# S4D convolution and gated GLU on one core: input spectrum moved once, exchanged copy on ScalarE, six more weight blocks on split parts

## The chip, the core and the metric

The kernel runs on one core of a Trainium2 chip. Its engines work side by side, each through its own list of instructions in a fixed order: TensorE (PE) multiplies, VectorE (DVE), ScalarE (ACT) and GpSimd (POOL) do elementwise work, SyncE (SP) issues the transfers between DRAM and the on-chip memory (SBUF; the products of PE land in PSUM). An instruction waits on semaphores for what it reads, and what stands behind it in its engine's list waits with it.

The metric is the time of one execution in device microseconds. A profiled execution gives the start and the duration of every instruction; the lines L1423 and so on are lines of the kernel's source.

## What is computed

A sequence of 2048 rows of 448 channels goes through a long convolution (a diagonal state space model, S4D) and through a gated linear unit; a sigmoid gate mixes the two.

```python
def _A_ref(u, log_A_real, A_imag, C_real, C_imag, log_dt, D_skip):
    ...
    P = jnp.exp((A * dt[:, None])[:, :, None] * pos[None, None, :])
    K = 2.0 * jnp.einsum("dn,dnl->dl", C, P).real
    ...
    Kf = jnp.fft.rfft(K, L2)
    Uf = jnp.fft.rfft(u_t, L2)
    y = jnp.fft.irfft(Uf * Kf[None, :, :], L2)[:, :, :L]
    ...
def _B_ref(x, w_gate, w_up, w_down):
    g = jnp.einsum("bsd,df->bsf", x, w_gate)
    u = jnp.einsum("bsd,df->bsf", x, w_up)
    h = _sigmoid(g) * u
    return jnp.einsum("bsf,fd->bsd", h, w_down)
...
g = _sigmoid((x * gate_w).sum(-1, keepdims=True))
return g * a + (1 - g) * b
```

Here D = 448, N = 256 states, L = 2048, and the hidden width of the unit is 1792 = 14 blocks of 128.

## The kernel before

**The convolution kernel K** is made in 28 chunks of 16 channels (`kgen`), each in two halves of 128 states (`half_chunk`). PE writes the angles to PSUM (L1232) and takes the whole turns off (L1241); ACT rounds and takes sines (L1236, L1238, L1243, L1244, L1254) into a tile `cs`; POOL raises powers in `tb`; DVE forms outer products of these (L1261, twice a half) and multiplies them into `cs` (L1275 and L1278). When both halves are done, PE sums over the states (L1290, 64 instructions), and ACT copies the sum out (L1311). There are three `cs` buffers. Below, "the first contraction" is L1290 of the first chunk, and the stages of the program are cut at the ends of the 1st, 9th, 20th and 28th contraction.

**The transforms** treat the 2048 rows as a matrix of 64 by 32. `Chain` holds one half of the channels: `stage1` (L812, L815), an exchange of axes (through DRAM, or on DVE, L826), `spectrum_four` (L845). For the input the spectrum is evacuated by ACT (L762) and stored in DRAM as `us` by `spectrum_u`. For the kernel there is one chain per half, tiles `fx_fu` and `fx_fk`; after the last chunk `product` goes through 8 blocks in each chain: it loads a block of `us` into a tile `ua` (`uax_fk` in the first chain, `ua_fk` in the second; two buffers each), DVE multiplies it by the kernel's spectrum straight from PSUM (L879), PE transforms back with 16 small matmuls (L889), and ACT evacuates (L762). `back` (L924, L928) makes the rows of the output.

A complex product needs real and imaginary parts against both parts of the other factor. In `us` the real parts lie in partitions 0 to 31 and 64 to 95 and the imaginary parts in the others. The kernel before writes two planes to DRAM: one with the real parts in the places of both, one with the imaginary parts in both (each transfer reads its source twice over), and `product` loads both planes of a block, in two transfers of 448 KB.

**The gated unit (GLU)** goes over 2 halves of the rows (H), 14 weight blocks (f) and 2 pieces of 512 rows (B). All operands are split in a rounded part and the rest, so that fast matmuls keep the precision. `glu_up` runs three matmuls for each of three pieces of the contraction and two for the fourth (L1423 to L1428), for gate and up; ACT takes the tanh (L1407), DVE forms the product with the up part. `glu_down` multiplies by the rows of `w_down`. Here stand two forms. For a block f that `WHOLE[H]` lists, DVE writes the product once as float32 (L1409), the weights are loaded as they are, and one float32 matmul of 448 columns is used (L1443; the profile has two records for each). For any other block DVE writes to `sg` (L1412), ACT makes the rounded part `hh` (L1414), DVE the rest `hl` (L1415), the weights are split too (L1388 on ACT, L1390 on DVE), and three fast matmuls are used (L1445, L1446, L1447). Results are scaled and added to `ob` by ACT (first group, L1455) or DVE (L1462).

**The order** is written out: the table `PLACE` gives, for each engine and each kind of tile, the places of its instructions in the engine's list. `Plan.order` merges these lists into one program; it can neither change the order on an engine nor skip a wait. So where a place in the table says that an instruction of ACT comes before another, it does, whether its input is there or not.

Of the kernel before, what the change touches and what calls it, by code (L numbers as in the profile page):

```python
# [13 lines left out]
AF = mybir.ActivationFunctionType  # L14
# [6 lines left out]
HD = 224  # L21
# [8 lines left out]
    ('Act', 'aci', 19): (65, 94,),  # L30
    ('Act', 'acr', 10): (15, 39, 49,),
    ('Act', 'acr', 19): (63, 91, 101,),
# [26 lines left out]
    ('Act', 'dots', 1): (28,),  # L59
    ('Act', 'dots', 2): (45,),  # L60
    ('Act', 'dots', 16): (67, 83,),
# [18 lines left out]
    ('Act', 'idn', 10): (12,),  # L80
    ('Act', 'junk', 10): (29, 60,),
    ('Act', 'junk', 19): (77, 81, 132,),
# [620 lines left out]
def gated_mix(ctx: ExitStack, tc, u, ut, aim, cre, cim, ldt, dskip, gw,  # L703
# [13 lines left out]
    def dt_(shape, name):  # L717
        return Res(name=name, real=dram.tile(list(shape), F32, name=name))
# [870 lines left out]
```

## Time and profile before

| what | value |
| --- | --- |
| three timed runs | 689.95, 688.12, 686.70 us; median 688.12 us |
| the profiled execution | 684.96 us |
| its span, first to last instruction | 683.0 us |
| mean granted TensorE clock | 0.999 |
| moved by DMA | 122.79 MB |

The profile's page lists the busy time of each engine, a chain of the work that ended last, and groups of instructions with their count, busy time and mean duration. A busy time is the union of the instructions' spans, and neighbours on DVE and ACT overlap a little, so that two of them in a row take less than the sum of their durations. For PE the ends are modelled, and the distance from one start to the next is the better measure. The windows give busy times of a stretch, with the number of records in brackets.

### The profile page before, as it was taken

The numbers are of one execution on the slowest core, as the hardware profiler recorded it, in microseconds if no ns is written. First come the engines' busy times: TensorE is split into PE (matmuls) and PEld (weight loads), VectorE is DVE, ScalarE is ACT, GpSimd is POOL, SyncE is SP. The second block draws the span as 40 slices with busy tenths as digits, with TensorE's granted clock in tenths as the row PEclk, the third lists the DMA queues.
The fourth block names the chain that finished last, engine by engine and source line by source line (L and its number), as shares of the span: only waits on it lengthen the run. The fifth ranks groups of instructions, "written<-read, shape, count | busy, mean of one in ns | idle before, by whom it ended". The sixth has DMA issues, their size and how long they took to land.

```text
span 683.0 us, 16235 instructions
## 1 busy us (share of the span) xinstructions
PE 669.7 (98%) x6568; PEld 480.6 (70%) x6568; DVE 603.7 (88%) x699; ACT 509.7 (75%) x928; POOL 269.2 (39%) x280
## 2 busy tenths in 40 slices
PE   8899999999999999999989999999999999999997
PEld 7677667877886687776646666778878766546864
DVE  7998999999899999999998999999974379667976
ACT  6588799898999999999999999999842442333110
POOL 0506486555466656675856567643000000000000
PEclk9999999999999999999999999999999999999999
DMA  8869432683793999737977884343968981888855
GB/s 265 222 146 245 111 101 57 174 217 139 208 173 85 204 203 225 237 111 178 176 211 179 200 212 113 124 155 111 204 133 217 280 292 66 300 276 217 153 141 129
DMA packets 96898, 122.79 MB, mean 180 GB/s; under 512 B 31032, under 2 KB 80504, under 8 KB 95800
## 3 DMA queue, kind: packets, MB, share of 16 engines
q1 hardware_dynamic: 96824, 121.76, 69.7%
q8 instruction: 52, 0.85, 0.5%
q14 instruction: 22, 0.18, 0.1%
HBM read 78.16 MB, written 43.58 MB: 178 GB/s over the span
## 4 chain that ended last, share of the span: by engine, by line
PE 82%; DVE 10%; ACT 3%; DMA 2%; issue 2%; SPq 1%; DVEq 0%
PE gu_gps L1423 10%; PE gu_gps L1424 9%; PE gu_gps L1425 9%; PE kp_egp L1290 7%; PE dn_gps L1443 6%; PE dn_gps L1445 5%; PE tp_egp L1232 4%; PE tp_egp L1241 4%; PE dn_gps L1446 4%; PE dn_gps L1447 4%; PE fps_fups L812 3%; PE gu_gps L1427 3%; PE fps_fups L845 3%; PE gu_gps L1428 3%; PE fps_fups L889 2%; PE fps_fkps L889 2%
## 5 line engine op out<-in xcount | busy, mean ns | idle before, releaser
L1423 PE MATMUL gu_gps<-xs_glu,wh_glu 128*128 128x512 f32 x336 | 144.6, 430 | 1.6 <-DVE hl_glu L1409 0.8
L1278 DVE TENSOR_TENSOR cs_eg<-cs_eg,es_eg 128x2048 f32<-128x2048 f32 x56 | 131.5, 2349 | 1.4
L1424 PE MATMUL gu_gps<-xs_glu,wh_glu 128*128 128x512 f32 x336 | 132.0, 393 | 0.1
L1425 PE MATMUL gu_gps<-xs_glu,wl_glu 128*128 128x512 f32 x336 | 131.7, 392 | 0.0
L1222 POOL TENSOR_TENSOR tb_eg<-tb_eg 128x96 f32<-128x96 f32 (+2 forms) x84 | 118.8, 1416 | 6.1
L1261 DVE TENSOR_TENSOR es_eg<-tb_eg 128x1024 f32<-128x1024 f32 x112 | 110.4, 1013 | 2.1 <-POOL tb_eg L1222 0.5
L1423 PEld LDWEIGHTS gu_gps<-xs_glu,wh_glu 128*128 128x128 f32 x336 | 63.2, 188 | 30.8 <-issue 15.8
L1275 DVE TENSOR_TENSOR cs_eg<-cs_eg,es_eg 128x1024 f32<-128x1024 f32 x56 | 70.8, 1264 | 8.2 <-ACT cs_eg L1254 5.8
L1238 ACT ACTIVATE nn_eg<-cs_eg 128x512 fp32r<-128x512 f32 x112 | 74.9, 669 | 3.8 <-PE tp_egp L1241 2.6
L1407 ACT ACTIVATE sg_glu<-gu_gps 128x512 f32<-128x512 f32 x56 | 34.5, 615 | 55.2 <-PE gu_gps L1428 54.9
L1424 PEld LDWEIGHTS gu_gps<-xs_glu,wh_glu 128*128 128x128 f32 x336 | 63.3, 188 | 16.0 <-issue 5.0
L1425 PEld LDWEIGHTS gu_gps<-xs_glu,wl_glu 128*128 128x128 f32 x336 | 63.1, 188 | 14.4
L1243 ACT ACTIVATE cs_eg<-tp_egp 128x512 f32<-128x512 f32 x112 | 70.0, 636 | 3.1 <-PE tp_egp L1241 2.7
L1236 ACT ACTIVATE cs_eg<-tp_egp 128x512 f32<-128x512 f32 x112 | 69.9, 633 | 2.7 <-PE tp_egp L1232 1.0
L1244 ACT ACTIVATE cs_eg<-tp_egp 128x512 f32<-128x512 f32 x112 | 69.0, 627 | 1.1 <-PE tp_egp L1241 1.1
L1254 ACT ACTIVATE cs_eg<-cs_eg,half_pi 128x1024 f32<-128x1024 f32 x56 | 66.7, 1191 | 0.2
L1225 POOL TENSOR_TENSOR tb_eg<-tb_eg,bs_eg 128x32 f32<-128x32 f32 x84 | 62.6, 745 | 6.4
L1462 DVE SCALAR_TENSOR_TENSOR ob_glu<-dn_gps,og,ob_glu 128x448 f32<-128x448 f32 x70 | 47.4, 677 | 16.0 <-PE dn_gps L1447 15.1
L1290 PEld LDWEIGHTS kp_egp<-cs_eg 128*32 128x32 f32 x3584 | 51.3, 110 | 10.7 <-issue 7.6
L1212 POOL MEMSET tb_eg<- 128x96 f32 x28 | 8.0, 287 | 127.9 <-DVE es_eg L1261 124.8
L1290 PE MATMUL kp_egp<-cs_eg 128*32 128x64 f32 x3584 | 55.8, 220 | 0.0
L1241 PE MATMUL tp_egp<-nn_eg,idn 128*128 128x512 f32 x112 | 51.4, 459 | 1.2 <-ACT nn_eg L1238 1.2
(168 smaller groups left out, 1326.0 us busy)
## 6 DMA issues: line engine op xcount, KB each, us to landing
shf<-fx_fu SPq DMA_DIRECT2D x16, 896.0 KB, 5.4
fx_fu<-shf SPq DMA_DIRECT2D x16, 896.0 KB, 10.4
us<-fx_fu SPq DMA_DIRECT2D x16, 896.0 KB, 9.7
xr_glu<-in_w_dram SPq DMA_DIRECT2D x46, 256.0 KB, 6.1
uax_fk<-us SPq DMA_DIRECT2D x16, 448.0 KB, 4.3
ua_fk<-us SPq DMA_DIRECT2D x16, 448.0 KB, 6.0
xr_glu<-in_w_dram SPq DMA_DIRECT2D x17, 224.0 KB, 4.1
gt_pre<-in_u_dram SPq DMA_DIRECT2D x8, 448.0 KB, 6.9
```

The costliest lines, as they stand in the source:

```text
L1222: pool(96 * m, lambda n=n, m=m: G.tensor_mul(g3(n + 1, m), g3(1, m), g3(n, 1).to_broadcast([128, 32, 3, m])))
L1236: op("Act", c_act(512, True), lambda: S.activation(cs[:, 1, ds, 32:96], block(tp), AF.Copy, bias=MAGIC), [tp], [(cs, ("s", i))], prio)
L1238: op("Act", c_act(512), lambda: S.activation(block(nn), cs[:, 1, ds, 32:96], AF.Copy, scale=-1.0, bias=MAGIC), [(cs, ("s", i))], [nn], prio)
L1241: op("PE", c_mm(532), lambda: T.matmul(tp.real, idn.real, nn.real, start=False, stop=True, skip_group_check=True), [nn, idn], [tp], prio)
L1243: op("Act", c_act(512, True), lambda: S.activation(cs[:, 0, ds, 32:96], block(tp), AF.Abs), [tp], [(cs, ("c", i))], prio)
L1261: V.tensor_mul(o.rearrange("p d (i k) -> p d i k", k=ny), x.unsqueeze(3).to_broadcast([128, 16, nx, ny]), y.unsqueeze(2).to_broadcast([128 ...
L1275: op("DVE", c_dve(1024), lambda: V.tensor_mul(cs[:, :, :, 0:32], cs[:, ::-1, :, 63:31:-1], es[:, :, 0:32].unsqueeze(1).to_broadcast([128, ...
L1278: op("DVE", c_dve(2048), lambda: V.tensor_mul(cs[:, :, :, 32:96], cs[:, :, :, 32:96], es[:, :, 32:96].unsqueeze(1).to_broadcast([128, 2, 1 ...
L1290: T.matmul(kp[32 * j:32 * j + 32, q], cs[:, z, 4 * j + q, 64:96], cs[:, z, 4 * j + q, 0:64], start=cs is parts[0] and z == 0 and q == 0, s ...
L1423: T.matmul(p.real, wh[:, k, cs], x[:, k], start=(k == 0), stop=False)
L1424: T.matmul(p.real, wh[:, k, cs], x[:, 4 + k], start=False, stop=False)
L1425: T.matmul(p.real, wl[:, k, cs], x[:, k], start=False, stop=False)
```

## The change

1. `spectrum_u` stores the spectrum once, as it lies in SBUF: 4 transfers a chain in place of 8, all of about 900 KB. `product` loads one plane of a block (one transfer of 448 KB in place of two). A new function `turn_parts` makes the second plane: for each of the two column groups z of a block, four ACTIVATE copies of 32 partitions by 448, each from one group of 32 partitions to its neighbour. That is 8 copies for a block and 128 in all. The matrices of the inverse transform change their signs to suit; sizes and numbers of the matmuls stay.
2. `WHOLE` loses blocks 11, 12 and 13 in both halves. Their 48 down products go from one float32 matmul to three of the split form. Each of the 12 pairs of block and piece gets an `hh` copy on ACT and an `hl` subtraction on DVE; the three weight blocks, shared by both halves, get a split on both engines.
3. All of `PLACE` is new.

```diff
 PLACE = {
...
-    ('Act', 'hh', 21): (237, 256, 268, 316, 333, 341,),
+    ('Act', 'hh', 21): (248, 265, 270, 318, 320, 344, 383, 401, 408, 483, 486, 494, 543, 551, 576, 647, 658, 663,),
...
-WHOLE = ((0, 1, 2, 3, 4, 11, 12, 13), (11, 12, 13))
+WHOLE = ((0, 1, 2, 3, 4), ())
...
-    turned[re], turned[im] = inv[im], -inv[re]
+    turned[re], turned[im] = inv[im], inv[im]
+    inv[im] = -inv[re]
...
-    us = [dt_([128, 2, 8, 2 * D], f"us{h}") for h in halves]
+    us = [dt_([128, 8, 2 * D], f"us{h}") for h in halves]
...
-            for q in range(2):
-                for g in range(2):
-                    for c in range(2):
-                        dma(lambda q=q, g=g, c=c: us[64 * g:64 * g + 64, c, 4 * q:4 * q + 4].rearrange(
-                                "(z k) b f -> k z (b f)", z=2),
-                            lambda q=q, g=g, c=c: x[64 * g + 32 * c:64 * g + 32 * c + 32, 16 * q:16 * q + 16].rearrange(
-                                "k l d -> k (l d)").unsqueeze(1).to_broadcast([32, 2, 8 * D]),
-                            64 * 16 * HD * 4, self.keys(8 * q, 8 * q + 8), [(us, (q, g, c))], prio, 215.0, 1400.0)
+            for q in range(4):
+                dma(lambda q=q: us[:, 2 * q:2 * q + 2].rearrange("p b f -> p (b f)"),
+                    lambda q=q: x[:, 8 * q:8 * q + 8].rearrange("p l d -> p (l d)"), 128 * 8 * HD * 4,
+                    self.keys(4 * q, 4 * q + 4), [(us, q)], prio)
...
                 ua = self.tile("ua", (128, 2, 2, D))
+                dma(lambda ua=ua: ua[:, 0].rearrange("p z f -> p (z f)"), lambda b=b: us[:, b], 128 * 2 * D * 4,
+                    [(us, b // 2)], [(ua, (0, 0)), (ua, (0, 1))], self.prio)
                 for c in range(2):
-                    dma(lambda ua=ua, c=c: ua[:, c].rearrange("p z f -> p (z f)"), lambda b=b, c=c: us[:, c, b],
-                        128 * 2 * D * 4, [(us, (b // 4, g, c)) for g in range(2)], [(ua, (c, 0)), (ua, (c, 1))], self.prio)
+                    self.turn_parts(ua, c)
                 self.product_four(ua, b)
 
+        def turn_parts(self, ua, z):
+
+            def f():
+                for a in range(0, 128, 32):
+                    to = a ^ 32
+                    S.activation(ua[to:to + 32, 1, z], ua[a:a + 32, 0, z], AF.Copy)
+            op("Act", 4 * c_act(D), f, [(ua, (0, z))], [(ua, (1, z))], self.prio)
```

In the changed kernel a line above the new function has a number lower by one than before, and a line below it a number higher by four: L1443 became L1447, L1415 became L1419.

The first place is DVE's list at the 19th chunk, both halves of it: `es` and `cs` belong to the kernel's generation, L1409 is the product of a whole block. Before:

```order
L1261 TENSOR_TENSOR es_eg_4445<-tb_eg_4240 128x16x64
L1261 TENSOR_TENSOR es_eg_4445<-tb_eg_4240 128x16x32
L1275 TENSOR_TENSOR cs_eg_4409<-cs_eg_4409,es_eg_4445 128x32x32
L1278 TENSOR_TENSOR cs_eg_4409<-cs_eg_4409,es_eg_4445 128x32x64
L1409 SCALAR_TENSOR_TENSOR hh_glu_4571<-sg_glu_4560,gu_gps_4422 128x512
L1261 TENSOR_TENSOR es_eg_4578<-tb_eg_4240 128x16x64
L1261 TENSOR_TENSOR es_eg_4578<-tb_eg_4240 128x16x32
L1275 TENSOR_TENSOR cs_eg_4528<-cs_eg_4528,es_eg_4578 128x32x32
L1278 TENSOR_TENSOR cs_eg_4528<-cs_eg_4528,es_eg_4578 128x32x64
```

In the changed kernel the list at the same chunk reads as follows; L1419 makes `hl`, and L1360 and L1361 split a piece of the input.

```order
L1419 TENSOR_TENSOR hl_glu_4548<-sg_glu_4085,hh_glu_4435 128x512
L1360 TENSOR_TENSOR xs_glu_3990<-xr_glu_3378,xs_glu_3990 128x256
L1361 TENSOR_TENSOR xs_glu_3990<-xr_glu_3378,xs_glu_3990 64x256
L1265 TENSOR_TENSOR es_eg_4624<-tb_eg_4343 128x16x64
L1419 TENSOR_TENSOR hl_glu_4642<-sg_glu_4439,hh_glu_4546 128x512
L1265 TENSOR_TENSOR es_eg_4624<-tb_eg_4343 128x16x32
L1279 TENSOR_TENSOR cs_eg_4479<-cs_eg_4479,es_eg_4624 128x32x32
L1282 TENSOR_TENSOR cs_eg_4479<-cs_eg_4479,es_eg_4624 128x32x64
L1265 TENSOR_TENSOR es_eg_4686<-tb_eg_4343 128x16x64
L1265 TENSOR_TENSOR es_eg_4686<-tb_eg_4343 128x16x32
L1279 TENSOR_TENSOR cs_eg_4633<-cs_eg_4633,es_eg_4686 128x32x32
L1282 TENSOR_TENSOR cs_eg_4633<-cs_eg_4633,es_eg_4686 128x32x64
```

Two subtractions, which the kernel before has nowhere between the 9th and the 20th contraction, stand in the first half of the chunk.

The second place is PE's list shortly ahead of the 19th contraction: `tp` and `nn` belong to the generation, `gu` to the up products, `dn` to the down products. Before:

```order
L1443 MATMUL dn_gps_4373<-vh_glu_3307,hh_glu_4571 128x448
L1241 MATMUL tp_egp_4585<-nn_eg_4605,idn 128x512
L1423 MATMUL gu_gps_4589<-xs_glu_3835,wh_glu_2408 128x512
L1424 MATMUL gu_gps_4589<-xs_glu_3835,wh_glu_2408 128x512
L1425 MATMUL gu_gps_4589<-xs_glu_3835,wl_glu_2424 128x512
```

And in the changed kernel:

```order
L1449 MATMUL dn_gps_4510<-vh_glu_3204,hh_glu_4546 128x448
L1450 MATMUL dn_gps_4510<-vh_glu_3204,hl_glu_4642 128x448
L1451 MATMUL dn_gps_4510<-vl_glu_3394,hh_glu_4546 128x448
L1236 MATMUL tp_egp_4709<-pos_sb,phs 128x512
L1245 MATMUL tp_egp_4683<-nn_eg_4704,idn 128x512
L1427 MATMUL gu_gps_4678<-xs_glu_3990,wh_glu_2793 128x512
```

The one float32 product is now three matmuls of the split form, and it reads `hl`, which the second subtraction above has made.

The third place is ACT's list in the middle of the products of the two chains. Before, evacuations follow one another, with a piece of the gated unit in between:

```order
L762 ACTIVATE fx_fk_6562<-fps_fkps_7023 128x448
L762 ACTIVATE fx_fk_6562<-fps_fkps_7022 128x448
L762 ACTIVATE fx_fu_5091<-fps_fups_7057 128x448
L762 ACTIVATE fx_fu_5091<-fps_fups_7056 128x448
L762 ACTIVATE fx_fk_6562<-fps_fkps_7070 128x448
L762 ACTIVATE fx_fk_6562<-fps_fkps_7069 128x448
L1407 ACTIVATE sg_glu_7132<-gu_gps_7005 128x512
```

In the changed kernel (evacuations are L761, the new copies L877):

```order
L877 ACTIVATE uax_fk_7173<-uax_fk_7173 32x448 x4
L761 ACTIVATE fx_fk_6687<-fps_fkps_7198 128x448
L877 ACTIVATE uax_fk_7173<-uax_fk_7173 32x448 x4
L1411 ACTIVATE sg_glu_7240<-gu_gps_7185 128x512
L761 ACTIVATE fx_fk_6687<-fps_fkps_7197 128x448
L877 ACTIVATE ua_fk_7216<-ua_fk_7216 32x448 x4
L761 ACTIVATE fx_fu_4915<-fps_fups_7244 128x448
L761 ACTIVATE fx_fu_4915<-fps_fups_7245 128x448
L877 ACTIVATE ua_fk_7216<-ua_fk_7216 32x448 x4
```

Eight copies for each block stand between the evacuations. The first of them wait for the block's transfer, and the evacuations behind them wait too.

How many instructions stand between the ends of the contractions 1, 9, 20 and 28, before and after, is this for the kinds that change on PE and DVE (instructions, not records). On PE the stages are cut behind the contraction, on DVE behind the last L1278 of the chunk.

| engine, kind | 1 to 9 | 9 to 20 | 20 to 28 | behind 28 |
| --- | --- | --- | --- | --- |
| PE whole down products (L1443) | 0, 0 | 31, 0 | 17, 0 | 0, 0 |
| PE split down products, three matmuls each | same | 9, 42 | 24, 39 | same |
| PE up products of 512 columns | -2 | +11 | -7 | -2 |
| PE angles of 512 columns (L1232) | same | +1 | -1 | same |
| PE spectrum matmuls (L845) | -4 | +4 | -4 | +4 |
| DVE `hl` subtractions (L1415) | 11, 10 | 0, 10 | 6, 9 | same |
| DVE splits of weights (L1390) | -1 | +4 (three of 448, one of 512) | same | same |
| DVE products L1409 and L1412 | same | 10, 11 | 9, 8 | same |

Ahead of the first contraction nothing changes in these numbers. Behind the 28th, DVE's list has the same kinds and numbers before and after, and ACT's has the 128 copies more. Behind the 9th contraction and up to the 28th, ACT gets the 12 `hh` copies and the three splits of weights.

More of the change, by code (lines that the diff above doesn't have):

```diff
@@ L29 @@
     ('Act', 'aci', 10): (14, 40,),
-    ('Act', 'aci', 19): (65, 94,),
-    ('Act', 'acr', 10): (15, 39, 49,),
-    ('Act', 'acr', 19): (63, 91, 101,),
[26 rows of a table removed]
-    ('Act', 'dots', 1): (28,),
+    ('Act', 'aci', 19): (61, 96,),
+    ('Act', 'acr', 10): (13, 39, 48,),
+    ('Act', 'acr', 19): (68, 91, 107,),
[26 rows of a table added]
+    ('Act', 'dots', 1): (29,),
     ('Act', 'dots', 2): (45,),
-    ('Act', 'dots', 16): (67, 83,),
[2 rows of a table removed]
+    ('Act', 'dots', 16): (66, 80,),
[2 rows of a table added]
     ('Act', 'ex1', 10): (21, 58,),
[15 rows of a table removed]
-    ('Act', 'idn', 10): (12,),
@@ L81 @@
-    ('Act', 'junk', 10): (29, 60,),
-    ('Act', 'junk', 19): (77, 81, 132,),
[12 rows of a table removed]
-    ('Act', 'pos_sb', 10): (36, 52,),
[13 rows of a table removed]
[15 rows of a table added]
+    ('Act', 'idn', 10): (15,),
+    ('Act', 'junk', 10): (33, 60,),
+    ('Act', 'junk', 19): (75, 81, 124,),
[12 rows of a table added]
+    ('Act', 'pos_sb', 10): (55, 36,),
[11 rows of a table added]
+    ('Act', 'uax', 40): (845, 843, 853, 849, 881, 882, 888, 886, 895, 897, 907, 906, 919, 917, 927, 926,),
[3 rows of a table added]
     ('Act', 'wh', 0): (1, 4,),
     ('Act', 'wh', 1): (6, 7,),
[4 rows of a table removed]
[4 rows of a table added]
     ('Act', 'xs', 0): (0, 2, 3, 5,),
[2 rows of a table removed]
-    ('DVE', 'aci', 10): (45,),
@@ L119 @@
-    ('DVE', 'aci', 19): (122,),
-    ('DVE', 'acr', 10): (89,),
-    ('DVE', 'acr', 19): (152,),
[15 rows of a table removed]
-    ('DVE', 'dtp', 10): (30,),
-    ('DVE', 'dtv', 10): (27,),
[14 rows of a table removed]
-    ('DVE', 'half_pi', 0): (9,),
[24 rows of a table removed]
-    ('DVE', 'ones', 10): (1,),
-    ('DVE', 'p', 10): (18, 20, 21, 22, 23, 25, 26,),
-    ('DVE', 'phs', 20): (2,),
[6 rows of a table removed]
-    ('DVE', 'skip', 20): (0,),
[6 rows of a table removed]
-    ('DVE', 'uax', 40): (539, 534, 546, 547, 556, 557, 570, 571, 578, 575, 585, 586, 590, 591, 595, 596, 624, 623,
[34 rows of a table removed]
[2 rows of a table added]
+    ('DVE', 'aci', 10): (42,),
+    ('DVE', 'aci', 19): (112,),
@@ L229 @@
+    ('DVE', 'acr', 10): (85,),
+    ('DVE', 'acr', 19): (152,),
[15 rows of a table added]
+    ('DVE', 'dtp', 10): (29,),
+    ('DVE', 'dtv', 10): (27,),
[14 rows of a table added]
+    ('DVE', 'half_pi', 0): (0,),
[23 rows of a table added]
+    ('DVE', 'ones', 10): (2,),
+    ('DVE', 'p', 10): (16, 17, 19, 21, 22, 23, 25,),
+    ('DVE', 'phs', 20): (1,),
[6 rows of a table added]
+    ('DVE', 'skip', 20): (3,),
[6 rows of a table added]
+    ('DVE', 'uax', 40): (547, 552, 561, 562, 576, 573, 586, 584, 593, 590, 597, 599, 604, 605, 610, 609, 639, 638,
[34 rows of a table added]
         1039,),
[2 rows of a table removed]
[2 rows of a table added]
         1041,),
[33 rows of a table removed]
[33 rows of a table added]
     ('Pool', 'bsx1', 10): (5, 11,),
     ('Pool', 'bsx1', 19): (17, 50,),
[2 rows of a table removed]
[2 rows of a table added]
```

523 rows, old and new, of the table PLACE are left out of this document.

## Prediction

> **What bounds the kernel now.** I read the page's head first, then its chain of work that ended last, then the table of windows cut at the stages.
>
> ```profile
> span 683.0 us, 16235 instructions
> PE 669.7 (98%) x6568; PEld 480.6 (70%) x6568; DVE 603.7 (88%) x699; ACT 509.7 (75%) x928; POOL 269.2 (39%) x280
> PE 82%; DVE 10%; ACT 3%; DMA 2%; issue 2%; SPq 1%; DVEq 0%
> 0.00:117.10 117.10, 111.66 (x556) 80.42 (x556) 108.61 (x195) 92.01 (x159) 55.52 (x54) 1.00 0.63 165
> 117.10:239.60 122.50, 122.50 (x1544) 93.00 (x1543) 119.00 (x118) 115.34 (x214) 69.51 (x73) 1.00 0.69 169
> 239.60:388.70 149.10, 146.95 (x1947) 101.16 (x1944) 143.47 (x129) 145.13 (x267) 95.20 (x98) 1.00 0.79 191
> 388.70:504.50 115.80, 115.78 (x1468) 88.22 (x1468) 109.06 (x102) 107.80 (x198) 49.00 (x56) 1.00 0.60 151
> ```
>
> The windows give stretch and length, then the busy time of PE, weight loads, DVE, ACT and POOL with their records, the granted clock (1.00 throughout), the DMA share and GB/s. I call the four stretches A, B, C, D, and what follows "late". PE is busy 98% of the span, and the chain lies on it for 82%. Work taken off PE therefore counts, unless another engine has no room. In C, DVE and ACT have only 149.10 - 143.47 = 5.6 us and 4.0 us of idle time; in D there are 6.7 and 8.0 us.
>
> **The down products: PE.** First the whole form in the chain, then split products and two matmuls of 512 columns in PE's timeline (start, duration).
>
> ```profile
> 399.70 0.75 PE dn_gps L1443 x2
> 632.05 0.36 PE L1445 MATMUL dn_gps<-vh_glu,hh_glu 128*128 128x448 f32 x1
> 632.65 0.36 PE L1445 MATMUL dn_gps<-vh_glu,hh_glu 128*128 128x448 f32 x1
> 633.26 0.40 PE L1427 MATMUL gu_gps<-xs_glu,wh_glu 128*128 128x512 f32 x1
> 633.49 0.39 PE L1428 MATMUL gu_gps<-xs_glu,wl_glu 128*128 128x512 f32 x1
> ```
>
> A whole product is two records and 0.75 us. A split one is the distance from one L1445 to the next, 0.605 us, since the ends are modelled. 48 products save 48 x 0.145 = 7.0 us of PE. A 512-column matmul costs 0.23 us.
>
> By the counts of the change, PE gets in C: -31 x 0.75 + 33 x 0.605 + 12 x 0.23 (up products, angles), and 0.8 for four spectrum matmuls at 0.20 = +0.3 us. In D: -17 x 0.75 + 15 x 0.605 - 8 x 0.23 - 0.8 = -6.3 us. B gets -1.3, late +0.3. So the saving doesn't fall where the whole products stood: C keeps its PE work, D loses 6.3.
>
> **The down products: DVE and ACT.** Groups (busy, mean ns, idle before), then DVE's timeline for the distance between neighbours.
>
> ```profile
> L1415 DVE TENSOR_TENSOR hl_glu<-sg_glu,hh_glu 128x512 fp32r<-128x512 f32 x34 | 25.0, 736 | 4.6 <-ACT hh_glu L1414 4.4
> L1390 DVE TENSOR_TENSOR vl_glu<-xr_glu,vh_glu 128x448 fp32r<-128x448 f32 x17 | 10.9, 652 | 1.9 <-ACT vh_glu L1388 1.9
> L1414 ACT ACTIVATE hh_glu<-sg_glu 128x512 fp32r<-128x512 f32 x34 | 22.3, 658 | 25.6 <-DVE sg_glu L1412 19.7 <-PE dn_gps L1447 6.0
> 371.77 0.69 DVE L1409 SCALAR_TENSOR_TENSOR hl_glu<-sg_glu,gu_gps 128x512 f32<-128x512 f32 x1 [0.32 <-ACT sg_glu L1407]
> 372.38 2.50 DVE L1261 TENSOR_TENSOR es_eg<-tb_eg 128x1024 f32<-128x1024 f32 x2
> ```
>
> A 512-column operation on DVE moves the next start by 372.38 - 371.77 = 0.61 us. C gets ten `hl`, one split of 512 columns and one product more (12 x 0.61) and three splits of 448 columns, which I estimate at 0.61 x 448/512 = 0.54: 7.3 + 1.6 = +8.9 us (by mean durations 10.9, an upper bound). DVE's work in C becomes 143.5 + 8.9 = 152.4 us, **more than the stage is long now**. D gets three `hl` more and one product less, 2 x 0.61 = +1.2, so 110.3 of 115.8 us. B loses one `hl` and one split, -1.3 with a little overlap, PE the same amount.
>
> ACT gets 12 `hh` (at most 12 x 0.66 by L1414's mean) and three splits, some 9 us. Counted by the stages of its new list, with the kinds at their mean durations, B loses 9 us, C gets 3 and D 7: 148.0 in C and 114.8 in D, each just inside the present length. C's lengthening by DVE therefore covers ACT, with no term of its own.
>
> How well can DVE be filled? The best stretch of the kernel before and C itself:
>
> ```profile
> 100.00:169.50 69.50, 69.50 (x796) 53.82 (x796) 68.68 (x72) 62.47 (x110) 41.35 (x41) 1.00 0.51 139
> 382.22 1.38 DVE L1275 TENSOR_TENSOR cs_eg<-cs_eg,es_eg 128x1024 f32<-128x1024 f32 x1 [0.38 <-ACT cs_eg L1254]
> 383.64 2.48 DVE L1278 TENSOR_TENSOR cs_eg<-cs_eg,es_eg 128x2048 f32<-128x2048 f32 x1
> 386.75 1.92 PE kp_egp L1290 x128
> DVE cs_eg L1275 <- ACT cs_eg L1254: 5.8, 11, 1.3
> ```
>
> The best share is 68.68/69.50 = 98.8%; C has 143.47/149.10 = 96.2%. The chunk shown is the 20th: DVE waits 0.38 us for ACT's sines, ends `cs` at 386.12, and PE's contraction starts at 386.75. The lead of DVE on PE is 0.6 us there, so a subtraction more in that half (the first place of the change) is a wait of PE unless DVE has been moved ahead earlier. The last row sums such waits on ACT between 169.5 and 500 us: 5.8 us in 11 (longest 1.3).
>
> So C takes 152.4/0.988 = 154.2 us at the best share, 152.4/0.962 = 158.4 at its own; against 149.1 that is +5.1 to +9.3. The lower bound is PE's own +0.3, if B's slack lets DVE run ahead by the rest; the upper one uses durations, +10.6. I take **+3.8** for C: near full DVE (152.9 us), since DVE can move idle time only across three `cs` buffers, and B gives it 1.3 us. For D the end of C leaves DVE with 110.3 to do: at 98.8% 111.6, -4.2; PE would allow -6.3; with C's 96.2% the stage would take 110.3/0.962 = 114.7, -1.1. I take **-4.4** (DVE at 99%). B: **-1.3**. A: same instructions in another order, **0** (2 either way, as its 5.4 us of PE idle time may shift).
>
> A page of the Trainium skill ("Perfetto Trace Analysis", section "Optimizing Scalar/DVE Operations") speaks against more subtractions. The rows first, the existing ones with their count and min/median/max, in D and then behind it, where POOL has nothing to do:
>
> ```profile
> L1415 DVE TENSOR_TENSOR hl_glu<-sg_glu,hh_glu x7: 678/686/778, 425.6 to 502.4; 128x512 fp32r<-128x512 f32 x7
> L1415 DVE TENSOR_TENSOR hl_glu<-sg_glu,hh_glu x15: 648/685/695, 506.8 to 670.9; 128x512 fp32r<-128x512 f32 x15
> ```
>
> The medians are 686 and 685 ns, so POOL beside it shows no effect but the one of 778. The page says that GpSimd and DVE share a read port, which some DVE operations hold alone, so that one stalls the other. By that, all twelve 512-column operations would be at 778 at worst, 12 x 0.09 = 1.1 us more in C, an estimate that gives 689.6. I go by the medians.
>
> **The moved spectrum and the copies.** DMA loses 8 transfers of `us` and 16 loads. What waited for them is one thing only:
>
> ```profile
>   DVE uax_fk L879: 2.8, 2
> DMA to landing us min/median/max: 2.3/3.3/5.4
> 499.63 0.58 ACT L1388 ACTIVATE vh_glu<-xr_glu 128x448 fp32r<-128x448 f32 x1 [1.51 <-PE dn_gps L1446]
> 500.64 1.03 ACT L1388 ACTIVATE vh_glu<-xr_glu 128x448 fp32r<-128x448 f32 x2
> 541.49 0.98 ACT L762 ACTIVATE fx_fu<-fps_fups 128x448 f32<-128x448 f32 x2 [0.69 <-PE fps_fups L889]
> 573.59 1.74 PE L889 MATMUL fps_fups<-uax_fk,m_sb 64*64 64x448 f32 x16
> 624.45 1.74 PE L889 MATMUL fps_fkps<-ua_fk,m_sb 64*64 64x448 f32 x16
> L879 DVE TENSOR_TENSOR uax_fk<-uax_fk,fps_fups x16: 1078/1083/1089, 529.5 to 614.9; 128x896 f32<-128x896 f32 x16
> 573.70:625.00 51.30, 51.30 (x400) 26.27 (x404) 35.60 (x41) 17.87 (x35) 0.00 (x0) 1.00 0.76 257
> ```
>
> DVE waited 2.8 us in two waits, and PE was busy through them (51.30 of 51.30), so the halved traffic gains nothing by itself: 0. The added copies have no row: 32 partitions by 448, so the nearest is a 448-column ACTIVATE of 128 partitions, one in 0.58 and two in 1.03 us, 0.45 from start to start; a quarter of the elements would give 0.11. I take 0.45, since the rows nearest in columns have it, and keep 0.11 for the range. Eight for a block are 3.6 us, 128 are 57.6. From the release of the third block's buffer to the last block, ACT has 80 copies, 36.0 us, and by the order 23 evacuations (0.44 by the second row of two: 0.98 less one of 0.54), two tanh and one `hh` (about 1.6 together): **47.7 us**, where it was busy 17.87 in 51.30.
>
> That is a loop: a buffer is free when PE's 16 matmuls are over (1.74), the load lands (3.3), ACT copies, DVE multiplies (1.08), PE goes on. From the third block's end to the last one's start, the ends 1.7 + 3.3 + 1.1 and the 47.7 make 53.8. PE itself goes from 573.59 to 624.45, 50.9 us, and by the order it has 11 matmuls of 512 columns more there (2.5), so 53.4. ACT would be late by 0.4 us plus whatever it idles. DVE's product has a second wait now, for the copies, and behind it in DVE's list stand the next block's product and `ob`; on ACT the evacuations stand behind a copy that waits for its load, and PE's next spectrum matmuls wait for those. I take +2.0 for this, with ends 0 (copies at 0.11) and +6 (a landing of 5.4 in place of 3.3 in about three of the loops). With PE's +0.3, **late is +2.3**.
>
> **The sum.** 0 - 1.3 + 3.8 - 4.4 + 2.3 = +0.4 us on the profiled execution, 684.96 us (its span 683.0 plus 2.0 around it): 685.4. The median of the three runs, 688.12, lies 3.16 us above that execution; with this added, **688.5 us**. 0.5% of it, 3.4 us, is about what a measurement of this kernel can tell from no change.
>
> **Rivals.**
> 1. *Faster, about 682 us.* DVE and ACT follow PE without idle time: the order puts DVE's extra work where B and D have slack (3.5 and 6.7 us), and the copies take less than 0.45. Then PE's -7.0 counts, less about 0.9 of waits: 688.1 - 6.1. For it: DVE over B to D has 119.0 + 143.5 + 109.1 - 1.3 + 8.9 + 1.2 = 380.4 us to do in 387.4, and PE's need becomes 380. Against it: DVE would have to be full all the way, and its lead is 0.6 us.
> 2. *Slower, about 694 us: DVE keeps its share in C.* The waits for ACT's sines stay (each subtraction also waits for its `hh`, 4.4 us in the existing ones), so C takes 158.4 us, +9.3 in place of +3.8: 688.5 + 5.5. It decides from a share below 97.8% on, a C longer than 155.9 us: 3.0 more than my 152.9 bring the sum from +0.4 to +3.4. Against it: 98.8% has been reached in a stretch with much the same chunks.
> 3. *Slower, about 692.5 us: ACT's copies lose 6 us rather than 2.* For it: loads land in up to 5.4 us, with two buffers only. Against it: the traffic is halved.
> 4. *The change doesn't do what it says:* halved traffic reaches no wait of PE; this is in every case above at 0.
>
> **How the numbers follow.** Forecast (saving given back, within 3.4 us of before) 0.38; rival 1 0.32; rival 2 0.20; rival 3 0.10. Faster 0.32, same 0.38, slower 0.30. The range goes from 681 (PE's full 7.0 kept: 688.1 - 7.0) to 695 (rival 2 with 1 us of rival 3), which leaves out some 0.2.
>
> **What would show it.** The contractions 1, 9, 20 and 28 end now at 117.1, 239.6, 388.7 and 504.5. I expect C at about 153 us with DVE at 99% and PE waiting several us for `cs` (L1282 of the changed kernel), D at 111 with PE full, and some us of PE waiting behind the copies (L877) between the first and last product. Copies spaced well under 0.4 us would make late 0. The prediction is wrong if C stays under 150 us with DVE full (rival 1), if DVE idles over 3.5 us in C (rival 2), or if `us` transfers turn out to have slowed other loads that PE waits for, of which this trace has none.

## The result and the profile after

| what | before | after |
| --- | --- | --- |
| median of the timed runs (4 each, same chip) | 689.04 us | 705.87 us (705.32 to 707.18) |
| ratio, 95% interval | | 1.0259 (1.0222 to 1.0296) |
| span of the profiled execution | 683.0 us | 703.2 us |
| contractions 1, 9, 20, 28 end | 117.1, 239.6, 388.7, 504.5 | 114.9, 238.7, 394.4, 507.2 |
| A, B, C, D, late | 117.1, 122.5, 149.1, 115.8, 178.5 | 114.9, 123.8, 155.7, 112.8, 196.0 |
| third `uax` product to last `ua` product | 573.6 to 624.5: 50.9 | 579.3 to 645.7: 66.4 |

The change makes the kernel 2.6% slower. By the two spans it is 20.2 us: 2.7 us are lost up to the 28th contraction and **17.5 us behind it**, 15.5 of them in the dense stretch of products. (The profiled execution of before lies below its median, so the medians differ by less, 16.8 us.)

The page of the changed kernel, its engines and the chain's shares:

```profile
span 703.2 us, 16465 instructions
PE 678.7 (97%) x6616; PEld 490.1 (70%) x6616; DVE 609.6 (87%) x714; ACT 585.8 (83%) x1069; POOL 275.3 (39%) x280
PE 49%; ACT 22%; DVE 13%; DMA 9%; issue 4%; POOL 2%; SPq 0%; DVEq 0%; ACTq 0%
```

ACT was 3% of the chain before and is 22% now. The windows of B, C, D and late (columns as in the prediction), and then the dense stretch, after and before:

```profile
114.90:238.70 123.80, 121.42 (x1540) 92.39 (x1536) 119.42 (x116) 115.89 (x213) 73.61 (x71) 1.00 0.59 156
238.70:394.40 155.70, 149.88 (x2005) 109.47 (x2001) 149.98 (x142) 151.89 (x283) 102.70 (x103) 1.00 0.63 166
394.40:507.20 112.80, 111.36 (x1470) 88.01 (x1466) 109.37 (x102) 107.71 (x199) 51.83 (x54) 1.00 0.49 123
507.20:703.20 196.00, 184.52 (x1070) 119.61 (x1067) 123.91 (x160) 122.20 (x221) 0.00 (x0) 0.98 0.58 150
```

```profile
579.30:645.70 66.40, 62.03 (x406) 29.87 (x405) 34.84 (x38) 62.10 (x113) 0.00 (x0) 0.97 0.40 129
```

```profile
573.60:624.50 50.90, 50.90 (x397) 26.09 (x396) 35.34 (x40) 17.87 (x35) 0.00 (x0) 1.00 0.76 257
```

In the stretch PE was never idle before (50.90 of 50.90). Now ACT is the full engine (62.10 of 66.40), PE idles 4.4 us, and its clock falls to 0.97. What one copy takes, by its line's group (min/median/max), and how copies stand in ACT's timeline:

```profile
L877 ACT ACTIVATE ua_fk<-ua_fk x64: 572/575/583, 545.0 to 644.3; 32x448 f32<-32x448 f32 x64
```

```profile
597.67 4.69 ACT L877 ACTIVATE uax_fk<-uax_fk 32x448 f32<-32x448 f32 x8
602.36 2.33 ACT L877 ACTIVATE ua_fk<-ua_fk 32x448 f32<-32x448 f32 x4
604.72 0.54 ACT L761 ACTIVATE fx_fk<-fps_fkps 128x448 f32<-128x448 f32 x1
605.29 2.33 ACT L877 ACTIVATE ua_fk<-ua_fk 32x448 f32<-32x448 f32 x4
```

Eight copies move the next start by 602.36 - 597.67 = 4.69 us, **0.586 each**. A copy lasts 0.575 us and overlaps with nothing, where the prediction had 0.45. The evacuation between two groups takes 605.29 - 604.72 = 0.57, where it had 0.44 ahead of another evacuation.

### The profile page after: what moved, and what is told of

Same layout as the page of the kernel before. It is cut to its first block, busy times and chain, and to the rows that moved or that the text cites. A ratio compares the mean times of both kernels' runs of the same rounds, so it can differ in the third digit from the quotient of the medians.

```text
span 703.2 us, 16465 instructions
## 1 busy us (share of the span) xinstructions
PE 678.7 (97%) x6616; PEld 490.1 (70%) x6616; DVE 609.6 (87%) x714; ACT 585.8 (83%) x1069; POOL 275.3 (39%) x280
## 4 chain that ended last, share of the span: by engine, by line
PE 49%; ACT 22%; DVE 13%; DMA 9%; issue 4%; POOL 2%; SPq 0%; DVEq 0%; ACTq 0%
PE gu_gps L1427 6%; PE gu_gps L1429 6%; PE gu_gps L1428 6%; PE kp_egp L1294 4%; PE dn_gps L1449 3%; PE dn_gps L1450 3%; PE dn_gps L1451 3%; ACT ua_fk L877 3%; DMA xr_glu<-in_w_dram 3%; ACT uax_fk L877 3%; DVE es_eg L1265 2%; PE dn_gps L1447 2%; PE tp_egp L1236 2%; ACT nn_eg L1242 2%; DVE cs_eg L1282 2%
## 5 line engine op out<-in xcount | busy, mean ns | idle before, releaser
L1282 DVE TENSOR_TENSOR cs_eg<-cs_eg,es_eg 128x2048 f32<-128x2048 f32 x56 | 130.7, 2333 | 1.2
L1226 POOL TENSOR_TENSOR tb_eg<-tb_eg 128x96 f32<-128x96 f32 (+2 forms) x84 | 106.2, 1265 | 5.9
L1229 POOL TENSOR_TENSOR tb_eg<-tb_eg,bs_eg 128x32 f32<-128x32 f32 x84 | 83.9, 999 | 6.2
L1427 PEld LDWEIGHTS gu_gps<-xs_glu,wh_glu 128*128 128x128 f32 x336 | 63.3, 188 | 27.6 <-issue 10.2
L1449 PE MATMUL dn_gps<-vh_glu,hh_glu 128*128 128x448 f32 x182 | 69.6, 383 | 1.9 <-issue 1.5
L1450 PE MATMUL dn_gps<-vh_glu,hl_glu 128*128 128x448 f32 x182 | 67.1, 368 | 0.0
L1451 PE MATMUL dn_gps<-vl_glu,hh_glu 128*128 128x448 f32 x182 | 66.6, 366 | 0.0
L1294 PEld LDWEIGHTS kp_egp<-cs_eg 128*32 128x32 f32 x3584 | 51.3, 110 | 10.6 <-issue 8.2
```

Source lines behind the costliest of these rows:

```text
L1226: pool(96 * m, lambda n=n, m=m: G.tensor_mul(g3(n + 1, m), g3(1, m), g3(n, 1).to_broadcast([128, 32, 3, m])))
L1229: pool(32, lambda e=e: G.tensor_mul(t(e + 1), t(e), b(3)))
L1282: op("DVE", c_dve(2048), lambda: V.tensor_mul(cs[:, :, :, 32:96], cs[:, :, :, 32:96], es[:, :, 32:96].unsqueeze(1).to_broadcast([128, 2, 1 ...
L1294: T.matmul(kp[32 * j:32 * j + 32, q], cs[:, z, 4 * j + q, 64:96], cs[:, z, 4 * j + q, 0:64], start=cs is parts[0] and z == 0 and q == 0, s ...
L1427: T.matmul(p.real, wh[:, k, cs], x[:, k], start=(k == 0), stop=False)
L1449: T.matmul(p[:, :D], hh[:, ts], vh.real, start=(i == 0), stop=False)
```

## The experiments

Theory 1: the 128 copies on ACT make ACT the bound of the late part. Rival: the new order of PE, DVE and SP makes the loss there. A second question is which engine makes C long. All medians stand beside runs of the kernel before on the same chip (its median lay between 688.4 and 690.2 us); "(one)" marks a single execution, which has no interval. The stages are those of the profiled execution. The first forms of short_copies2 and pool_copies2 left no time.

| run | C | D | late | stretch | median, or single time |
| --- | --- | --- | --- | --- | --- |
| before | 149.1 | 115.8 | 178.5 | 50.9 | 689.04 |
| after | 155.7 | 112.8 | 196.0 | 66.4 | 705.87 |
| two_loads | 173.5 | 125.7 | 183.7 | 54.0 | 725.01 |
| dma_exchange | 156.8 | 112.9 | 189.2 | 55.2 | 701.16 |
| short_copies2 | 157.4 | 112.7 | 185.4 | 56.0 | 697.70 (one) |
| pool_copies2 | 155.4 | 112.8 | 183.5 | 56.9 | 694.16 |
| copy_forms | 156.1 | 112.8 | 181.8 | 55.2 | 695.82 (one) |
| before_copies | 148.8 | 115.8 | 222.5 | 83.3 | 728.45 |
| before_pool | 148.9 | 115.8 | 196.0 | 69.0 | 704.05 |
| pool_hh | 155.8 | 113.6 | 183.5 | 57.0 | 693.19 (one) |
| pool_hl | 160.6 | 120.0 | 182.8 | | 704.66 (one) |
| pool_both | 161.5 | 119.5 | 183.4 | | 706.91 |
| hl_copy | 158.0 | 112.8 | 182.9 | | 700.28 (one) |
| two_products | 158.7 | 117.8 | 184.1 | | 703.31 (one) |

### The copies taken off ACT

**two_loads** puts the old path of the spectrum into the changed kernel:

```diff
-            for q in range(4):
-                dma(lambda q=q: us[:, 2 * q:2 * q + 2].rearrange("p b f -> p (b f)"),
...
+            for q in range(2):
+                for g in range(2):
+                    for c in range(2):
...
-                    self.turn_parts(ua, c)
+                    dma(lambda ua=ua, c=c: ua[:, c].rearrange("p z f -> p (z f)"), lambda b=b, c=c: us[:, c, b],
...
```

> The changed kernel with the spectrum's old path: two planes stored, two loads for each block, no copies on ACT; the rest of the order and the split weight blocks as in the changed kernel. Theory 1 (the 128 copies at 0.585 us make ACT the bound behind the 28th contraction): the part behind the 28th contraction falls from 196.0 to 178-182 us, the median from 705.9 to 688-692; between the 9th and the 20th contraction the loss of 6.6 us against the kernel before stays (155-157 us). Rival (the new order of PE and DVE makes the loss there): the late part stays above 190 us, the median above 700.

Late came out at 183.7 us, as theory 1 has it, but the whole at 725.01: C and D grew by 17.8 and 12.9 us. ACT's and SP's timelines of that run show a reason (SP's rows are its queue's):

```profile
264.37 0.63 ACT L1391 ACTIVATE wh_glu<-xr_glu 128x512 fp32r<-128x512 f32 x1 [12.09 <-DMA xr_glu<-in_w_dram]
```

```profile
244.57 5.52 SPq L715 DMA_DIRECT2D us<-fx_fu  x4
250.19 2.41 SPq L715 DMA_DIRECT2D xr_glu<-in_w_dram  x1
263.91 0.67 SPq L715 DMA_DIRECT2D fx_fu<-in_u_dram  x1
264.68 0.55 SPq L715 DMA_DIRECT2D xr_glu<-in_w_dram  x1
```

Behind the four stores, SP has a load into `fx_fu` (263.91), the buffer that they read. Here SP issues nothing between 252.6 and 263.9, and the weight load for which ACT waits 12.09 us stands behind. The same happens once more in D, where ACT waits 12.21 us, and the clock was 0.94 in C and 0.96 in D. That is the cost of eight stores at the places of four, not of the kernel before, and the next run avoids it.

**dma_exchange** keeps the stores and the first load of the changed kernel and fills the second plane by four loads of 32 partitions:

```diff
-                for c in range(2):
-                    self.turn_parts(ua, c)
+                for a in range(0, 128, 32):
+                    to = a ^ 32
+                    dma(lambda ua=ua, to=to: ua[to:to + 32, 1].rearrange("p z f -> p (z f)"), lambda b=b, a=a: us[a:a + 32, b],
...
```

> The changed kernel with the second plane filled by four small loads for each block, from the one plane that is stored, in place of the copies on ACT; the stores and everything up to the 28th contraction stay. This keeps the transfers ahead of that point, which the run with two stored planes had not: there ACT waited 12 us twice for a weight load that stood behind the stores. Theory 1 (the copies on ACT are the bound of the late part): the 28th contraction ends at 507 us (2 either way), the late part falls from 196.0 to 180-185 us, the median from 705.9 to 690-695. Rival (the order of the other instructions makes the loss): late stays above 192 us.

The stretch fell from 66.4 to 55.2 us, so theory 1 holds there. Late is 189.2, between the two numbers, since the part ahead of the third `uax` product grew from 72.1 to 76.7 us. Its longest wait of PE there (total, times, longest) is for a transfer of the kernel's rows:

```profile
PE fps_fkps L814 <- DMA fx_fk<-kd: 3.4, 1, 3.4
```

The clock in this part was 0.96, which is 0.04 x 76.7 = 3.1 us (an estimate). The ratio to before is 1.0139 (1.0095 to 1.0182).

**short_copies2** keeps every wait and the order, with a quarter of each copy; for the rest of the second plane the load of a block fills both planes:

```diff
-                    S.activation(ua[to:to + 32, 1, z], ua[a:a + 32, 0, z], AF.Copy)
+                    S.activation(ua[to:to + 32, 1, z, :112], ua[a:a + 32, 0, z, :112], AF.Copy)
...
```

> The changed kernel with copies of 112 of the 448 columns on ACT; for the rest one load fills both planes alike, so three quarters of the exchange are left out. All waits for copies and the order stay. Theory 1: a copy falls from 0.575 to about 0.25 us, ACT's 80 copies of the dense stretch from 46.8 to some 20 us, and the late part from 196.0 to 178-184 us. Rival (the waits, not the copies' length): the late part stays above 190 us.

A copy took 0.295 us, the stretch 56.0 us, late 185.4. The waits are the same and 10.6 of the 17.5 us are gone, so most of the loss was ACT's work, and not the added step between load and product.

**pool_copies2** moves the copies to POOL:

```diff
-                    S.activation(ua[to:to + 32, 1, z], ua[a:a + 32, 0, z], AF.Copy)
+                    G.tensor_copy(ua[to:to + 32, 1, z], ua[a:a + 32, 0, z])
...
```

> The changed kernel with the 128 copies on POOL, which has nothing to do behind the 28th contraction, in the same sequence. Theory 1: ACT is relieved, and the late part follows POOL's price of a copy, which no row shows: at up to 0.6 us each the 80 copies of the dense stretch take 48 us beside 53 us of PE, late 180-188 us; at 1.2 us POOL is the bound with 96 us there, late over 220 us. Rival (the waits and not an engine's work): late stays at 196 us.

The copy's group on POOL, and the stretch in that run:

```profile
L879 POOL COPY ua_fk<-ua_fk x64: 550/555/922, 547.9 to 635.9; 32x448 f32<-32x448 f32 x64
```

```profile
581.90:638.80 56.90, 55.23 (x408) 27.59 (x407) 36.04 (x40) 17.50 (x35) 44.70 (x80) 1.00 0.48 151
```

The 80 copies are 44.70 us of POOL in a stretch of 56.90, ACT is back at 17.50, and late is 183.5: nearly the 183.7 without any copy. The median falls by 11.7 us to 694.16, 1.0072 (1.0040 to 1.0104) of before. It is the best of the variants with a measured interval, and still not better than before.

### Part 1 in the order of before

**before_copies** and **before_pool** put the one plane, the one load and the copies (on ACT, on POOL) into the kernel before, at the places that they have in the changed kernel against the instructions behind them.

```diff
                 ua = self.tile("ua", (128, 2, 2, D))
+                dma(lambda ua=ua: ua[:, 0].rearrange("p z f -> p (z f)"), lambda b=b: us[:, b], 128 * 2 * D * 4,
...
                 for c in range(2):
-                    dma(lambda ua=ua, c=c: ua[:, c].rearrange("p z f -> p (z f)"), lambda b=b, c=c: us[:, c, b],
+                    self.turn_parts(ua, c)
...
```

> The kernel before with part 1 alone: one plane, one load for each block, 128 copies on ACT at the places that they have in the changed kernel against the evacuations behind them; whole weight blocks and the order of before otherwise. Theory 1: the stages up to the 28th contraction stay as before (504.5 us, 2 either way), the late part grows from 178.5 by 14-20 us, the median to 703-710. Rival (the new order is the cause): the late part stays under 184 us, the median under 695.

> The kernel before with part 1 alone and its 128 copies on POOL, at the places of the run with part 1 alone on ACT (728.5 us). If the copies cost only where they stand on ACT: late part 178-184 us in place of 222.5, median 688-694 us, and the halved traffic brings nothing. If the added step from load to product costs by itself: late above 190 us.

Up to the 28th contraction nothing moved beyond 3 us (505.3 and 507.1 against 504.5), so the halved traffic brings nothing there. Late grew by 44.0 us on ACT, over twice what was expected, and by 17.5 on POOL: in the order of before, the added step costs also where POOL makes the copies, against the expectation of 178-184. The stretch of before_pool:

```profile
576.20:645.20 69.00, 58.77 (x397) 27.58 (x396) 36.46 (x40) 17.96 (x35) 45.79 (x80) 0.93 0.43 131
```

PE idles 10.2 us there, against 1.7 in pool_copies2, and at a clock of 0.93 another 0.07 x 69 = 4.8 us are lost (an estimate). The loads are not issued late: in the stretch of both runs SP issues each within 0.2 us of the end of the matmuls that free its buffer. What in the new order makes room for the added step was not followed up. The places of the copies were mine, so neither 44.0 nor 17.5 is the least that part 1 costs in that order.

### Why a copy takes 0.59 us

**copy_forms** takes four forms of the copy in turn over the blocks:

```diff
...
+                if form == 3:
+                    S.activation(ua[:, 1, z], ua[:, 0, z], AF.Copy)
+                    return
+                if form == 2:
+                    for a in range(0, 128, 64):
+                        S.activation(ua[a:a + 64, 1, z], ua[a:a + 64, 0, z], AF.Copy)
+                    return
                 for a in range(0, 128, 32):
-                    to = a ^ 32
+                    to = a ^ 32 if form == 0 else a
```

> The changed kernel with four forms of the copy, block by block in turn: 4 x 32 partitions exchanged as in the changed kernel; 4 x 32 partitions to the same partitions; 2 x 64 partitions to the same; 1 x 128 partitions to the same. The last three leave out the exchange. It measures why a copy costs 0.585 us from start to start where the 448-column ACTIVATE of 128 partitions costs 0.45. Theory a (the exchange of partitions): only the first form costs 0.58, the others 0.45. Theory b (32 partitions): the first two cost 0.58. Theory c (input and output in one tile): all four cost 0.58 where two stand in a row. The late part gets shorter than 196.0 us since ACT has 22 copies for four blocks in place of 32.

ACT's timeline with the 32, 64 and 128 partition forms (L884, L880, L876):

```profile
597.49 4.69 ACT L884 ACTIVATE uax_fk<-uax_fk 32x448 f32<-32x448 f32 x8
602.20 0.58 ACT L876 ACTIVATE ua_fk<-ua_fk 128x448 f32<-128x448 f32 x1
```

```profile
593.11 1.16 ACT L880 ACTIVATE ua_fk<-ua_fk 64x448 f32<-64x448 f32 x2
594.29 0.98 ACT L761 ACTIVATE fx_fu<-fps_fups 128x448 f32<-128x448 f32 x2
```

```profile
603.68 0.57 ACT L876 ACTIVATE ua_fk<-ua_fk 128x448 f32<-128x448 f32 x1
604.15 0.53 ACT L761 ACTIVATE fx_fk<-fps_fkps 128x448 f32<-128x448 f32 x1
```

The durations are equal, 0.57 to 0.58 us. But 32 partitions take 4.71/8 = 0.589 from start to start, exchanged or not, and 64 take 1.18/2 = 0.59, while the one with 128 lets the next begin after 0.47. None of the three theories had it quite: neither the exchange nor the shared tile is the reason, and not 32 partitions alone.

Nor is it that a copy covers a part of the partitions. ACT's list in the kernel before has instructions on 112 partitions that overlap with their neighbours, and in copy_forms the first copy of a block without the exchange (L884, partitions 0 to 31) begins before the evacuation ahead of it has ended:

```profile
99.16 0.62 ACT L1069 ACTIVATE hi_pro<-acr_pro 112x512 fp32r<-112x512 f32 x1
99.69 0.58 ACT L1236 ACTIVATE cs_eg<-tp_egp 128x512 f32<-128x512 f32 x1
```

```profile
542.38 0.53 ACT L814 ACTIVATE fx_fk<-fps_fkps 128x448 f32<-128x448 f32 x1
542.80 2.32 ACT L884 ACTIVATE uax_fk<-uax_fk 32x448 f32<-32x448 f32 x4
```

L1069 has the next start after 0.53 us at a duration of 0.62, the evacuation after 0.42 at 0.53. What these four have in common is that all start at partition 0. The copies of 32 and 64 partitions start at 0, 32, 64 and 96 in turn. **An ACTIVATE whose input or output in SBUF starts at another partition than the last one that ACT read or wrote there began only after the instruction ahead had ended**: so it was, without exception, behind the 28th contraction in copy_forms and in the changed kernel. It also fits the evacuation ahead of an exchanged copy (0.57 us to the next start in place of 0.44), since the first exchanged copy writes from partition 32. No run has copies of 32 partitions that start at one partition all along.

### Which engine makes C long

Five runs on top of pool_copies2 (C 155.4): the twelve added `hh` copies on POOL (**pool_hh**), the twelve `hl` subtractions there (**pool_hl**), both (**pool_both**); and, on DVE and PE, **hl_copy** and **two_products**.

```diff
+        if f in (11, 12, 13):
+            op("Pool", c_pool1(512), lambda: G.tensor_copy(hh.real, sg.real), [sg], [hh], prio)
+        else:
+            op("Act", c_act(512), lambda: S.activation(hh.real, sg.real, AF.Copy), [sg], [hh], prio)
...
```

> The run with the exchange copies on POOL, and the twelve added hh copies (blocks 11 to 13) on POOL as well. It asks which engine binds between the 9th and the 20th contraction (C), where the changed kernel has ACT busy 151.9 and DVE 150.0 of 155.7 us and PE needs about 147.3. If ACT binds: ACT loses 4.8 us there, C falls from 155.4 to 150-152 us. If DVE binds: C stays at 155-157 us. POOL is busy 105 us there and has some 45 us of waiting for DVE.

> The run with the exchange copies on POOL, and the twelve added hl subtractions on POOL as well. If DVE binds in C: DVE loses 5.8 us there, C falls from 155.4 to 149-152 us. If ACT binds: C stays at 155-157 us. A subtraction on POOL has no row; if it takes over 1 us, the powers that POOL raises come later, and C grows.

> Both: the exchange copies, the twelve added hh copies and the twelve added hl subtractions on POOL. If ACT and DVE bind together in C, only this run reaches PE's need: C at 148-150 us, the 28th contraction at 500-505 us, the median at 683-689 us. If the order of the changed kernel itself is what costs (waits back and forth between PE, ACT and DVE), C stays above 153 us.

C in the first two runs:

```profile
238.50:394.30 155.80, 149.03 (x2001) 110.00 (x2001) 153.68 (x142) 148.50 (x274) 115.35 (x112) 1.00 0.63 166
```

```profile
239.50:400.10 160.60, 152.78 (x2002) 110.90 (x2001) 150.87 (x133) 152.35 (x283) 115.01 (x112) 0.97 0.62 161
```

With the `hh` copies gone ACT fell to 148.50 us, and C stayed: DVE filled up to 153.68 instead, with the same 142 instructions. In pool_hl DVE had nine instructions fewer (133) and no less busy time (150.87 against 149.98 in the changed kernel). So DVE's operations grew longer while POOL did more (the 22 products of 128 x 1024 into `cs` had a mean of 1.245 us in pool_copies2 and 1.342 in pool_hl), and this experiment does not relieve DVE; it also put PE behind POOL, whose subtractions took 1.9 us in the median. pool_both (161.5) fails in the same way.

The two other edits:

```diff
+            if f in (11, 12, 13):
+                V.tensor_copy(hl.real, hh.real)
+            else:
+                V.tensor_sub(hl.real, sg.real, hh.real.bitcast(F32))
```

```diff
+            if fs[i] in (11, 12, 13):
+                T.matmul(p[:, :D], hl[:, ts], vl.real, start=False, stop=(i == len(fs) - 1))
+                return
```

> The run with the exchange copies on POOL, in which the twelve added hl subtractions on DVE become copies of hh into hl: the subtraction is left out, the instruction still waits for hh and still writes hl, but reads one tile where the subtraction reads two. A copy's duration has no row here; by the subtraction's own 0.7 us it saves up to about 0.35 us each, 3.5 us of DVE between the 9th and the 20th contraction (C). If DVE binds C: C falls from 155.4 to 151-153 us. If PE with its waits for ACT binds: C stays at 155-157 us.

> The run with the exchange copies on POOL, in which the down products of blocks 11, 12 and 13 take two matmuls in place of three (one of the small terms is left out, all tiles are still read): 0.20 us of PE less for each of 33 products in C, 6.6 us, and 3.0 us less between the 20th and the 28th contraction (D). If PE's own work binds C: C falls from 155.4 to 149-151 us. If DVE and ACT bind it: C stays at 154-156 us and PE idles more; D likewise stays at 112-113 us.

C in both, and PE's longest pause in the second:

```profile
244.60:402.60 158.00, 152.47 (x2005) 111.05 (x2001) 148.96 (x142) 152.70 (x283) 94.01 (x103) 0.98 0.63 164
```

```profile
240.30:399.00 158.70, 146.03 (x1968) 104.03 (x1968) 149.18 (x142) 151.86 (x283) 99.91 (x103) 0.98 0.62 163
```

```profile
356.54 0.58 PE L1434 MATMUL gu_gps<-xs_glu,wl_glu 128*128 128x512 f32 x1 [6.49 <-issue]
```

Neither got shorter. Both ran C at a clock of 0.98, which is 0.02 x 158 = 3 us (an estimate), and two_products has a pause of 6.49 us for which the profile names no releaser. Without that pause its C would be 152.2 us (an estimate), of which ACT is busy 151.86. So taking 6.6 us of PE away would gain some 3 us, and then ACT is full. That is consistent with three engines being nearly full at once in C. Which single wait decides is **not settled**: every relief was clouded by the clock, the pause or the neighbour.

## Why the prediction was wrong, step by step

**The copy's price is the step that failed.** The prediction said "I take 0.45, since the rows nearest in columns have it, and keep 0.11 for the range". It measured 0.586. The same row had the right upper end beside it, its duration of 0.58 us, if the overlap with the neighbour is not taken for granted. The loop itself was right: its 80 copies at 0.586 are 46.9 us, the other ACT work 11.7, the ends 6.1, together 64.7 against the measured 66.4. (In the trace 3.6 us lie between the third block's matmuls and the first copy, then 60.3 with ACT busy 58.8, up to the end of the last copy; the evacuations ahead of copies take more than the 0.44 of the forecast, too.) At 0.45 it was 53.8, beside PE's 53.4, so that the two looked even; nearly a third more per copy is almost all loss.

| term | predicted | measured |
| --- | --- | --- |
| A | 0 | -2.2 |
| B | -1.3 | +1.3 |
| C | +3.8 (+0.3 to +10.6) | +6.6 |
| D | -4.4 (-6.3 to -1.1) | -3.0 |
| late | +2.3 (0.3 to 6.3) | +17.5 |
| sum | +0.4 | +20.2 |

*PE's share of late was right.* The 11 extra matmuls of the stretch made 50.9 + 2.5 = 53.4; without copies on an engine it takes 54.0 (two_loads). Of the 17.5 us, 12.3 go when the copies are gone (183.7). The other 5.2 are 3.1 in the stretch, where the forecast had 2.5 for the moved matmuls, 3.0 ahead of the third block and -1.0 behind the last. The 3.0 are not the order's alone: pool_copies2 has the same order and takes 69.6 us there, 0.6 more than before.

*Part of the loss is the clock, which the prediction left out.* PE's timeline after one of the waits behind copies, and windows of 1.70 us around it:

```profile
624.12 0.97 PE L844 MATMUL fps_fkps<-fx_fk,m_sb 64*64 64x448 f32 x4 [2.12 <-ACT fx_fk L761]
```

```profile
621.40:623.10 1.70, 0.60 (x6) 0.00 (x0) 0.00 (x0) 1.65 (x4) 0.00 (x0) 1.00 0.79 129
623.10:624.80 1.70, 0.68 (x4) 0.20 (x4) 1.13 (x2) 1.66 (x4) 0.00 (x0) 1.00 1.04 424
624.80:626.50 1.70, 1.70 (x6) 1.19 (x5) 1.58 (x3) 1.64 (x4) 0.00 (x0) 0.56 0.63 262
626.50:628.20 1.70, 1.70 (x6) 1.53 (x5) 1.70 (x2) 1.68 (x3) 0.00 (x0) 0.50 0.00 0
```

PE waits 2.12 us for an evacuation that stands behind copies, and then for 3.4 us its clock is 0.50 to 0.56: another 1.6 us lost. The Trainium skill ("TensorE: Matmul & The Clock Gate", Part 1 on the HAM clock gate) has PE at half rate after an idle window of about 3.4 us. The trace agrees on the half rate, but here a pause of 2.12 us was enough, with PE busy 1.28 of the 3.40 us ahead of it.

*C: the wait that was expected did not come.* The forecast had DVE nearly full and PE waiting for `cs` (L1282). DVE's share stayed at 96.3% (149.98 of 155.70; before 96.2%), which is what rival 2 described, with less work than I gave it (+6.5 in place of +8.9). But PE's longest waits in C are these (total, times, longest):

```profile
PE tp_egp L1245 <- ACT nn_eg L1242: 1.6, 7, 0.4
PE dn_gps L1449 <- issue: 1.5, 1, 1.5
PE fps_fups L844 <- DMA fx_fu<-shf: 1.2, 1, 1.2
```

ACT is named for 2.7 us in all, a transfer for 1.2, and DVE for none. PE idled 3.7 us more than before and was busy for 2.9 more, where the counts gave +0.3; why the busy time grew stays open. ACT's +3 in C was too small: 145.13 became 151.89, +6.8, so C had two nearly full engines and not one; in B and D, where I had -9 and +7, ACT's busy time stayed within 0.6 us. C's +6.6 lies between the forecast and rival 2, inside the bounds, but PE's waits were not those of the forecast: the size is partly luck. (The upper bound itself, +10.6, does not follow from its numbers: 10.9 us more at a share of 96.2% give +11.4.)

*B and D.* B came out at +1.3 in place of -1.3: PE idled 2.4 us there, 1.9 of them for a load of the input (`fx_fu<-in_u_dram`). D gave back 3.0 in place of 4.4, with one wait of 1.2 us for ACT.

*The port.* The prediction went by the medians against the rule of the Trainium skill ("Perfetto Trace Analysis", section "Optimizing Scalar/DVE Operations") that GpSimd and DVE share a read port. pool_hl agrees with the rule: more work on POOL, and DVE as busy with nine instructions fewer. In the change itself POOL has the same 280 instructions, and the subtractions in C had a median of 0.685 us, as I took it.

*Transfers.* "Gains nothing by itself" held: up to the 28th contraction before_pool and before_copies are not shorter than before.

*The rivals.* Rival 3 (copies lose more on ACT) named the right place at a third of its size; none of the cases reached 706.

## What to carry to other kernels

An instruction's start-to-start distance may be taken from a row only where its neighbours, its shape and the partition at which it starts are those of the row; otherwise its full duration is nearer. Where two engines come out within a few per cent of each other in one stretch, the sum is not a forecast but a threshold: carry the price error of the denser one through the whole count, here 80 instructions times 0.14 us. Work that must be added to a dense stretch belongs on the engine that idles there, and the step it adds must fit the order: with the copies on POOL, late grew by 5.0 us in the new order and by 17.5 in the old one.

## What the runs showed of the hardware

- A copy of 448 columns by ACTIVATE has one duration for 32, 64 and 128 partitions (0.57 to 0.58 us), and the next one begins before it ends (0.47 us from start to start) where both start at the same partition, and not (0.59) where the start changes from one to the next.
- POOL copied 32 x 448 in a median of 0.555 us (0.550 to 0.922, pool_copies2), ACT in 0.575.
- A pause of PE of 2.12 us was followed by 3.4 us at half clock.
- A DVE copy of 128 x 512 took 0.428 us in the median (hl_copy) where the subtraction of two tiles takes 0.685.
